# Attention and a gated unit on one core: K and Q loaded as one tile of nine tokens a partition, engines from a list, and a last output tile in quarters

## The chip, the cores and the metric

One core of a Trainium2 chip. The metric is the time of one execution on the device in microseconds; lower is better. The core has five engines with a queue of instructions each: TensorE (PE; its weight loads are listed apart as PEld), VectorE (DVE), ScalarE (ACT), GpSimd (POOL) and SyncE (SP), which here issues the transfers, and 16 DMA engines that carry them out. PE writes to PSUM, eight banks of 128 partitions x 512 fp32; all else is in SBUF, 128 partitions.

## What is computed

```python
def _attn_ref(q, k, v):                    # 8 batches, 8 heads, 576 positions, 64 dims, fp32
    scores = scale * np.matmul(q, k.transpose(0, 1, 3, 2))
    mask = block_i >= block_j              # blocks of 64 positions
    attn = np.exp(np.where(mask, scores, -1e9) - row_max);  attn /= attn.sum(-1)
    return np.matmul(attn, v)

def _moe_ref(x, w_val, conv_w, w_out):     # x: (8, 576, 512); conv_w: (5, 512)
    for k in range(5): gate_pre += conv_w[k] * xp[:, k:k + S, :]     # causal, along positions
    return (sigmoid(gate_pre) * (x @ w_val)) @ w_out
```

The attention's output, the eight heads side by side as 512 columns, goes through a depthwise convolution of five taps, a sigmoid gate, and two projections of 512 x 512.

## The kernel before

Work goes by 32 *pairs* of heads, four to a batch. Each step is an entry in a `Planner` (lines 40 to 166): the engines that may do it with a cost for each, its needs, and the PSUM banks that it holds. PE's steps stand in the order of the string `ORDER` (line 21), written out beforehand; `plan()` walks through all engines with the costs and gives every other step the engine that would be done with it first, and a place in that engine's queue. So the program that is built has a fixed order for each engine. Letters of `ORDER`, with the lines of what they emit:

- **T** (`transposes`, 326): K and Q of a pair, cast to fp16, are turned so that dims lie on partitions, 16 transposes of 64 rows for positions 0 to 511 and 2 for the *tail*, positions 512 to 575.
- **S** (`scores`, 375), three to a pair: scores by blocks, the masked ones left out, 22 matmuls in all. ACT takes exp of each two banks (`exps`, line 415, 128 x 1024).
- **P** (`products`, 438): 30 matmuls of 65 columns, V with a column of ones. DVE takes the reciprocal of the sums (463) and multiplies (473).
- **X** (`xt_steps`, 479): ten transposes back, evicted by `evict_x` (496). **G** (`gate`, 502): the convolution as 20 matmuls with diagonal weights, then tanh on ACT (519). **V** (`val`, 524), eight to a batch: x @ w_val, multiplied with the gate on DVE (`gated`, 540).
- **O** (`out_tile`, 546): 18 tiles of 128 output positions, each 16 matmuls of 512 columns into two banks, evicted with a factor 0.5 (`evict_out`, 563, 128 x 1024) and stored (574); a tile that crosses a batch's edge is stored in two pieces of its rows. **f** is a flag over the sums' range, **c** the convolution weights' transposes.

Loads go through SP in the planner's order (the first of Q through ACT). For a pair: K and Q of positions 0 to 511, each 128 partitions x 2 heads x 4 consecutive positions, so runs of 1 KB (262); V as two loads in runs of 256 B (303). For a batch: three tails of eight heads in runs of 256 B (310): K's to partitions 0-63, Q's to 64-127, V's. w_val and w_out come in eight loads into borrowed buffers (719), and the second half of w_out by a copy within SBUF (729). Rings: 5 raw tiles, 4 casts, 5 transposed K/Q tiles, 3 output buffers (`NOB`). Casts to fp16 stand at line 317: K's and Q's, V's and the tails' on POOL, but for the first pair or two. The transposed K is evicted with a stride of 64 elements on the PSUM side (357), since a partition holds four positions; Q needs none, as its transposes write to strided places (366). X therefore uses a permuted identity (`perm16`, 274). On POOL alone also stand a copy of a K block (`dup`), of a probability block (`keep_last`, 422), and two clearings of masked halves (`zeros`, 434).

The last steps: five O one after another, then f; the last O is evicted in two halves of 128 x 512, each stored by itself. Behind everything the flag is read, and a branch to an exact path (`exact_path`) that these data do not take.

Of the kernel before, what the change touches and what calls it, by code (L numbers as in the profile page):

```python
# [21 lines left out]
    "TTSTTSSSSTSSSSTPScXSPTSGPSTXSSPSSTSGXPGSSXTXPSGGXSSPSTGXSSTSGPSVVVVTSSVVVXVSTSPS"  # L22
    "SPVVVVXSPVVGTSXVVSSPGGXTSXGTSSGPSVVSSTVSVXSVVSTSPPSSVVTSPXXGGSXGGTSPSSVVVVXSTSPS"
    "SOSTOXSOSTPPSSVVVXSTGVSSXPGSTSPGGSTOSTOXSVVVVVTSSPPXSGGXSVVXSSOSTVVVSSPGGSTSPPSS"
    "VVVVVVXSOSTOSTOXXOSSPPGGGTSSOXSOSSOSPPPXXVVVXXVVVVGGGGGVVVVVVVVVOOOOOf")
# [14 lines left out]
class Planner:  # L40


    def __init__(self):
        self.steps = []

    def add(self, kind, key, engines, emit, needs=(), mode=None, banks=0, size=None, apart=False):
        s = Step(kind, key, engines, emit, needs, mode, banks, size, apart)
        s.n = len(self.steps)
        self.steps.append(s)
        return s  # L50

    def rank(self):
# [13 lines left out]
        for s in reversed(self.steps):  # L66
            if "PE" not in s.engines:
                s.rank = s.held.rank + 7 if s.held is not None else len(ORDER)
        changed = True
        while changed:  # L70
            changed = False
            for s in self.steps:
                for d in s.needs:
                    if "PE" not in d.engines and d.rank > s.rank:
                        d.rank = s.rank
                        changed = True

    def plan(self):
# [15 lines left out]
        def release(s):  # L94
            s.at = max([0.0] + [d.land for d in s.needs])
            if "PE" in s.engines:
                s.engine, s.ready = "PE", True
                return
            s.engine = min(s.engines, key=lambda e: (max(free[e], s.at) + s.engines[e], e))
            ready[s.engine].append(s)  # L100
# [69 lines left out]
def kernel(  # L170
# [46 lines left out]
    perm16 = ring(1, [128, 64], fp16, "perm16")[0]  # L217
# [6 lines left out]
    NRAW, NC, NT, NV, NPT, NX, NXT, NTH, NOB = 5, 4, 5, 6, 4, 3, 3, 9, 3  # L224
# [3 lines left out]
    tail32 = ring(2, [128, 8, 64], fp32, "tail32")  # L228
    tail16 = ring(2, [128, 8, 64], fp16, "tail16")
# [4 lines left out]
    kqs = ring(NT, [128, 1280], fp16, "kq")  # L234
# [23 lines left out]

    def load_runs(engine, src, t, b, j):
        engine.dma_start(
            out=t[:, :, :, :].rearrange("p e t d -> p e (t d)"),
            in_=src[b, 2 * j:2 * j + 2, 0:512, :].rearrange("e (p t) d -> p e (t d)", t=4))

    load_runs(nc.sync, k, raws["k"][0], 0, 0)
    load_runs(nc.scalar, q, raws["q"][0], 0, 0)
# [4 lines left out]
    for r in range(2):  # L272
        rows = slice(64 * r, 64 * r + 64)
        nc.vector.tensor_copy(out=perm16[rows, :].rearrange("p (s t) -> p t s", t=4),
                              in_=ident[rows, rows].rearrange("p (t s) -> p t s", t=4))
# [6 lines left out]
    RUN = {1024: 290.0, 256: 185.0, 2048: 340.0}  # L282
# [8 lines left out]
    def load_qk(p, name):  # L291
        b, j = divmod(p, PPB)
        src, t = {"k": k, "q": q}[name], raws[name][p % NRAW]
        return load(p - 4 + (0.1 if name == "q" else 0),
                    lambda _: load_runs(nc.sync, src, t, b, j), 262144, RUN[1024],
                    before(p - NRAW, "c" + name), 470)

    def load_v(p, e):
        b, j = divmod(p, PPB)
        t = raws["v"][p % NRAW]  # L300
# [7 lines left out]
    def load_tail(b, src, t, rows, users):  # L308
        def emit(_):
            nc.sync.dma_start(out=t[rows, :, :],  # L310
                              in_=src[b, :, 512:576, :].rearrange("h p d -> p h d"))

        return load(PPB * b - 3.8, emit, 131072, RUN[256], users, 650)

# [6 lines left out]
    def cast_engines(p, name):  # L321
        if p == 0:
            return {"DVE": 430} if name == "k" else {"ACT": 600}
        return {"POOL": 613} if p > 1 else {"POOL": 613, "DVE": 430}

    def transposes(p, parts):
        b, j = divmod(p, PPB)
        c16 = {n: casts[n][p % NC] for n in ("k", "q")}
        t16 = tail16[b % 2]

        def emit(s):
            i = s.group[0]
            for name, at in (("k", 320), ("q", 64)):
                if name not in parts:
                    continue
                for t in range(4):
                    for r in range(2):
                        rows = slice(64 * r, 64 * r + 64)
                        o = ps16[:, i + r, at:at + 256]
                        if name == "k":  # L340
                            o = o[:, 64 * t:64 * t + 64]
                        else:
                            o = o.rearrange("p (n t s) -> p t n s", t=4, s=16)[:, t, :, :]
                        nc.tensor.transpose(out=o, in_=c16[name][rows, t, :, :],  # L344
                                            identity=ident16[rows, rows])
            for r in range(2):
                rows = slice(64 * r, 64 * r + 64)
                if "t" in parts:
                    nc.tensor.transpose(out=ps16[:, i + r, 0:64], in_=t16[rows, 2 * j:2 * j + 2, :],  # L349
                                        identity=ident16[rows, rows])  # L350

        return emit

    def evict_k(p, tr):
        def emit(s):
            i = tr.group[0]
            copier(s.engine)(  # L357
                out=kqs[p % NT][:, 768:1280].rearrange("p (r s t) -> p r s t", r=2, t=4),
                in_=ps16[:, i:i + 2, 320:576].rearrange("p r (t s) -> p r s t", t=4))

        return emit

    def evict_q(p, tr, lo, hi):
        def emit(s):
            i = tr.group[0]
            copier(s.engine)(  # L366
                out=kqs[p % NT][:, 128:768].rearrange("p (r x) -> p r x", r=2)[:, :, lo:hi],
                in_=ps16[:, i:i + 2, lo:hi])

        return emit  # L370
# [4 lines left out]
    def scores(p, c):  # L375
        K = kqs[p % NT]
        TWICE, ZERO, KEYS, LAST = 0, 64, 768, 448

        def emit(s):
            i = s.group[0]  # L380

            def group(off, key, q0, n, start=True, stop=True):
                for e in range(2):
                    r = slice(64 * e, 64 * e + 64)
                    mm(out=ps[:, i + e, off:off + n], lhsT=K[r, key:key + 128],
                       rhs=K[r, q0:q0 + n], start=start, stop=stop)

            def both_halves(off, key):
                for e in range(2):
                    r = slice(64 * e, 64 * e + 64)  # L390
                    mm(out=ps[:, i + e, off:off + 512], lhsT=K[r, key:key + 128],
                       rhs=K[r, 128:768].rearrange("p (h x) -> p h x", h=2)[:, :, 64:320])

            if c == 0:
                both_halves(0, KEYS)
            elif c == 1:
                group(0, KEYS + 128, 320, 128)
                group(128, KEYS + 128, 512, 256)
                group(384, TWICE, 640, 64, stop=False)
                group(384, ZERO, LAST, 64, start=False)  # L400
                group(448, KEYS + 384, 704, 64)
            else:
                group(0, KEYS + 256, 512, 256)
                for tt in range(4):
                    group(256 + 64 * tt, KEYS + 128 * tt, LAST, 64)
# [14 lines left out]
    def keep_last(p):  # L420
        def emit(_):
            nc.gpsimd.tensor_copy(  # L422
# [5 lines left out]
    def zeros(p, first):  # L428
        def emit(_):
# [4 lines left out]
            nc.gpsimd.memset(seg[:, :, :, 0:64], 0.0)  # L434
# [44 lines left out]
    def xt_steps(p):  # L479
        def emit(s):  # L480
            for c in range(5):
                for r in range(2):
# [4 lines left out]
                        identity=perm16[rows, :] if c < 4 else ident16[rows, rows])  # L487
# [58 lines left out]
    def out_tile(i):  # L546
        def emit(s):
            for n in range(8):
                for e in range(2):
                    rows = slice(64 * e, 64 * e + 64)  # L550
                    mm(out=ps[:, s.group[0] + e, :], lhsT=gv[rows, n, 128 * i:128 * i + 128],
                       rhs=w_out_sb[rows, n, :], start=(n == 0), stop=(n == 7))
# [3 lines left out]
    def evict_out(n, ot, half=None):  # L556
        h = slice(0, 2) if half is None else slice(half, half + 1)

        def emit(s):
            i = ot.group[0]  # L560
            o, x = obs[n % NOB][:, h, :], ps[:, i + h.start:i + h.stop, :]
# [7 lines left out]
    def store(n, b, x0, x1, half=None):  # L569
        at = HALF * (b % UNIT) - 128 * (n % TILES)  # L570
        h = slice(0, 2) if half is None else slice(half, half + 1)

        def emit(_):
            nc.sync.dma_start(
                out=out[b, :, :].rearrange("(e s) n -> s e n", e=2)[x0:x1, h, :],
                in_=obs[n % NOB][at + x0:at + x1, h, :])
# [8 lines left out]

    def holds(s, *users):
# [3 lines left out]
    def memsets(key, engines, todo):  # L590

        def emit(s):
            e = {"DVE": nc.vector, "POOL": nc.gpsimd}[s.engine]
            for t, x in todo:
                e.memset(t, x)
# [26 lines left out]
    first = {n: add("", -4, {e: 0}, lambda _: None, size=(262144, RUN[1024]))  # L622
# [344 lines left out]
```

## Time and profile before

| | |
|---|---|
| median of 3 runs | 195.76 us (193.81 to 197.12) |
| the profiled execution | 194.38 us, of which the span of instructions is 192.6 us |
| busy: PE / DVE / ACT / POOL | 168.8 / 120.4 / 132.1 / 101.1 us |
| first matmul, first V step, last matmul | 4.5, 43.0, 184.3 us |
| mean granted clock of TensorE | 0.986 |

Times in the profile are microseconds from the span's start. A group's row has: line, engine, operation, out<-in with partitions x elements and type, count, then busy time, mean ns of one, and the idle time of the engine just before with what ended it. A timeline row: start, length, engine, line, operation, count. A row of the windows: the stretch and its length, busy time and count of PE, PEld, DVE, ACT and POOL, granted clock, mean busy share of the DMA engines (over 1 where packets overlap) and GB/s. Matmuls are pipelined, so the length of a matmul row reaches into the next; the time from start to start is the price.

### The profile page before, as it was taken

To read this page: it belongs to the slowest core of one execution; us is meant where nothing else is said; L and a number is where in the kernel's file an instruction comes from. 1 tells how busy PE (TensorE), PEld (TensorE's weight loads), DVE (VectorE), ACT (ScalarE), POOL (GpSimd) and SP (SyncE) were. 2 spreads that over 40 slices of the span, in tenths; PEclk is the share of its full clock that TensorE was granted. 3 is DMA by queue.
4 is the path that set the end of the run, shared out by engine and by line. 5 is a ranking of instruction groups with operands and counts; after the bars stand their busy time and mean duration, and the time that the engine had idled before them with its cause. 6 is when DMAs were issued, how large, how long until landed. Compare 5 with 4: busy or idle time off the path is not lost.

```text
span 192.6 us, 9420 instructions
## 1 busy us (share of the span) xinstructions
PE 168.8 (88%) x4006; PEld 127.4 (66%) x4006; DVE 120.4 (63%) x271; ACT 132.1 (69%) x151; POOL 101.1 (53%) x251
## 2 busy tenths in 40 slices
PE   0678789989999979997999979999999999999930
PEld 0357667868887758866577847868855858886410
DVE  6727877599798868958449727846944524965000
ACT  3398597995729978687787947798667997061540
POOL 4296977857855668774866855659642121000000
PEclk9999999999999999999999999999999999999995
DMA  5999998999998899999999999999837425200692
GB/s 153 315 235 171 285 233 221 277 331 185 233 252 189 239 212 228 234 205 206 228 226 238 300 348 264 245 299 331 194 122 245 181 90 145 101 3 3 158 333 67
DMA packets 70633, 41.05 MB, mean 213 GB/s; under 512 B 48053, under 2 KB 64949, under 8 KB 70586
## 3 DMA queue, kind: packets, MB, share of 16 engines
q1 hardware_dynamic: 70314, 40.13, 82.9%
q8 instruction: 33, 0.54, 1.2%
q10 hardware_dynamic: 272, 0.26, 0.4%
q14 instruction: 14, 0.11, 0.2%
HBM read 30.42 MB, written 9.44 MB: 207 GB/s over the span
## 4 chain that ended last, share of the span: by engine, by line
PE 52%; DMA 24%; ACT 6%; DVE 5%; POOL 5%; issue 3%; SPq 2%; POOLq 0%; ACTq 0%; DVEq 0%
PE ps L195 47%; DMA tail<-in_q_dram 8%; DMA qraw<-in_q_dram 8%; ACT pt L415 4%; DMA vraw<-in_v_dram 4%; DMA kraw<-in_k_dram 2%; DMA out_dram<-ob 2%; PE ps L344 2%; PE ps L484 2%; POOL ve L317 2%; ACT ob L563 2%; DVE xn L473 1%; DVE kq L357 1%; POOL qc L317 1%; DVE kq L366 1%
## 5 line engine op out<-in xcount | busy, mean ns | idle before, releaser
L415 ACT ACTIVATE pt<-ps 128x1024 f16<-128x1024 f32 x96 | 94.0, 1026 | 28.4 <-PE ps L195 20.1
L195 PE MATMUL ps<-kq 64*128 64x64 f16 (+3 forms) x704 | 36.4, 233 | 2.1 <-DVE kq L366 1.9
L357 DVE COPY kq<-ps 128x512 f16<-128x512 f16 x32 | 22.1, 690 | 23.5 <-PE ps L349 18.8
L195 PE MATMUL ps<-ve,pt 128*128 128x65 f16 x896 | 33.5, 195 | 2.7 <-POOL ve L317 1.7
L195 PE MATMUL ps<-xt,w_val 128*64 128x288 f16 x512 | 35.4, 288 | 0.3 <-DVE xn L473 0.3
L195 PE MATMUL ps<-w_out,gv 64*128 64x512 f16 x288 | 33.4, 376 | 1.2 <-ACT pt L415 1.2
L195 PEld LDWEIGHTS <-pt 128*128 128x128 f16 x896 | 30.8, 98 | 5.1 <-issue 2.0
L195 PEld LDWEIGHTS <-w_val 128*64 128x64 f16 x512 | 27.4, 110 | 4.7 <-issue 2.1
L195 PEld LDWEIGHTS <-kq 64*128 64x128 f16 x704 | 23.1, 98 | 11.1 <-issue 4.3
L540 DVE SCALAR_TENSOR_TENSOR gv<-th,ps 128x288 f16<-128x288 f32 x64 | 27.7, 452 | 4.0 <-ACT th L519 1.5
L519 ACT ACTIVATE th<-ps 128x576 f32<-128x576 f32 x32 | 20.2, 653 | 10.5 <-PE ps L195 10.4
L473 DVE TENSOR_TENSOR xn<-ps,rinv 128x640 f16<-128x640 f32 x32 | 26.3, 823 | 1.0
L563 ACT ACTIVATE ob<-ps 128x1024 f32<-128x1024 f32 (+1 forms) x19 | 18.5, 980 | 11.8 <-PE ps L195 9.4
L195 PE MATMUL ps<-xt,diag 64*64 64x288 f16 x640 | 23.5, 285 | 0.7 <-ACT pt L415 0.7
L195 PEld LDWEIGHTS <-gv 64*128 64x128 f16 x288 | 13.5, 94 | 15.1 <-issue 1.5
L434 POOL MEMSET pt<- 64x256 f16 x64 | 19.7, 312 | 5.6 <-ACT pt L415 4.0
L317 POOL CAST ve<-vraw 128x512 f16<-128x512 f32 x32 | 19.5, 614 | 4.7 <-DMA vraw<-in_v_dram 3.5
L317 POOL CAST kc<-kraw 128x512 f16<-128x512 f32 x30 | 18.4, 614 | 5.1 <-DMA kraw<-in_k_dram 3.9
L317 POOL CAST qc<-qraw 128x512 f16<-128x512 f32 x30 | 18.3, 612 | 4.8 <-DMA qraw<-in_q_dram 3.1
L422 POOL COPY pd<-pt 64x128 f16<-64x128 f16 x32 | 9.6, 299 | 20.8 <-ACT pt L415 20.0
L496 DVE COPY xt<-ps 128x640 f16<-128x640 f16 x31 | 14.9, 485 | 7.1 <-PE ps L484 6.9
L195 PEld LDWEIGHTS <-diag 64*64 64x64 f16 x640 | 17.1, 106 | 2.9 <-issue 1.1
(53 smaller groups left out, 143.4 us busy)
## 6 DMA issues: line engine op xcount, KB each, us to landing
kraw<-in_k_dram SPq DMA_DIRECT2D x32, 256.0 KB, 5.1
vraw<-in_v_dram SPq DMA_DIRECT2D x64, 128.0 KB, 5.1
qraw<-in_q_dram SPq DMA_DIRECT2D x31, 256.0 KB, 5.6
out_dram<-ob SPq DMA_DIRECT2D x11, 512.0 KB, 3.4
out_dram<-ob SPq DMA_DIRECT2D x4, 384.0 KB, 4.2
out_dram<-ob SPq DMA_DIRECT2D x6, 256.0 KB, 4.7
tail<-in_k_dram SPq DMA_DIRECT2D x8, 128.0 KB, 5.3
tail<-in_q_dram SPq DMA_DIRECT2D x8, 128.0 KB, 5.3
```

The source lines that it names most:

```text
L195: nc.tensor.matmul(out=out, lhsT=lhsT, rhs=rhs, start=start, stop=stop, skip_group_check=True)
L317: copier(s.engine)(out=out, in_=in_)
L344: nc.tensor.transpose(out=o, in_=c16[name][rows, t, :, :], identity=ident16[rows, rows])
L357: copier(s.engine)(out=kqs[p % NT][:, 768:1280].rearrange("p (r s t) -> p r s t", r=2, t=4), in_=ps16[:, i:i + 2, 320:576].rearrange("p r ...
L415: nc.scalar.activation(out=heads(p)[:, :, 512 * c:512 * c + 512], in_=ps[:, i:i + 2, :], func=AF.Exp, bias=0.0, scale=0.125)
L422: nc.gpsimd.tensor_copy(out=pds[p % NPT][64:128, 0:128].rearrange("p (e x) -> p e x", e=2), in_=heads(p)[64:128, :, COL[3]:COL[3] + 64])
L434: nc.gpsimd.memset(seg[:, :, :, 0:64], 0.0)
L473: nc.vector.tensor_tensor(out=xns[p % NX][:, :, :, :].rearrange("p c e d -> p e c d"), in0=o[:, :, :, 0:64], in1=ri.to_broadcast([128, 2, ...
L496: copier(s.engine)(out=xts[b % NXT][:, g, PAD:PAD + 640].rearrange("p (c r x) -> p r c x", r=2, x=64), in_=ps16[:, i:i + 2, 0:320].rearran ...
L519: nc.scalar.activation(out=ths[p % NTH][:, :, :], in_=ps[:, i:i + 2, 0:HALF], func=AF.Tanh, bias=0.0, scale=0.5)
L540: nc.vector.scalar_tensor_tensor(out=gv[:, 2 * g + r, s0:s0 + HALF], in0=ths[(PPB * b + g) % NTH][:, r, :], scalar=1.0, in1=ps[:, va.group ...
L563: nc.scalar.activation(out=o, in_=x, func=AF.Copy, bias=0.0, scale=0.5)
```

## The change

- **One tile for K and Q.** K goes to partitions 0-63, Q to 64-127, each partition with nine consecutive positions (64 x 9 = 576), in runs of 2304 B; the tails of K and Q go (16 loads of 128 KB), V's stay. One cast a pair of 128 x 1152 elements instead of two of 512 and a share of the tail's (for the first pair K's on DVE, Q's on ACT). T is again 18 transposes of 64 rows. Both evictions are now 128 x 576 with a stride, on DVE or ACT, and put positions back in order, so `perm16` goes and the scores take queries in one piece: two matmuls of 128 and 256 columns for each head become one of 384, 20 matmuls a pair.
- **Engines from a list.** A step that more than one engine may do takes it from the string `CHOICE` (320 letters) and not from the planner. `keep_last`, `zeros`, `dup` and V's casts may now be DVE's; `evict_kq` and the output evictions are shared. Counts in the built programs:

| | before | after |
|---|---|---|
| K/Q casts | POOL 60, DVE 3, ACT 1, tails 8 | POOL 22, DVE 10, ACT 1 |
| K/Q evictions | DVE 65 | DVE 43, ACT 21 |
| xt evictions | DVE 31, ACT 1 | DVE 23, ACT 9 |
| V casts / `dup` / `keep_last` / `zeros` on DVE | none | 12 / 11 / 15 / 31 |
| output evictions | ACT 17 + 2 halves | ACT 7 + 1 quarter, DVE 10 + 3 quarters |
| transfers of K and Q with tails | 64 + 16 | 64 |

- **A new `ORDER`**, with 122 changes between forms of matmul where there were 118. The first V stands at place 47, before at place 63; ahead of it stand 9 T, 23 S, 6 P, 4 X and 4 G, before 12, 28, 8, 7 and 7. In SP's queue 16 loads of K or Q and 14 of 256 B runs stand ahead of the last of w_val, before 20 and 24.
- **The end.** The last O becomes two steps of 256 columns, evicted in quarters of 128 x 256, each stored by itself (128 KB). f is now ahead of them, and they need the flag. `NOB` is 4.

```diff
+CHOICE = ("PADPDDDDDDDDPPPDDPDDDPPDPDPP..." )
...
+        s.engine = next(iter(engines))
+        if len(engines) > 1:
+            s.engine = {"D": "DVE", "A": "ACT", "P": "POOL"}[CHOICE[self.choices]]
+            self.choices += 1
...
-            s.engine = min(s.engines, key=lambda e: (max(free[e], s.at) + s.engines[e], e))
...
-    raws = {n: ring(NRAW, [128, 2, 4, 64], fp32, n + "raw") for n in ("k", "q", "v")}
-    casts = {n: ring(NC, [128, 4, 2, 64], fp16, n + "c16") for n in ("k", "q")}
+    raws = ring(NRAW, [128, 2, 9, 64], fp32, "kqraw")
+    casts = ring(NC, [128, 9, 2, 64], fp16, "kq16")
+    vraws = ring(NRAW, [128, 2, 4, 64], fp32, "vraw")
...
+    def load_runs(engine, n, t, b, j):
+        engine.dma_start(
+            out=t[64 * n:64 * n + 64, :, :, :].rearrange("p e t d -> p e (t d)"),
+            in_=(k, q)[n][b, 2 * j:2 * j + 2, :, :].rearrange("e (p t) d -> p e (t d)", t=9))
...
+            for t in range(9):
+                for r in parts:
+                    rows = slice(64 * r, 64 * r + 64)
+                    nc.tensor.transpose(
+                        out=ps16[:, s.group[0] + r - parts[0], 64 * t:64 * t + 64],
+                        in_=casts[p % NC][rows, t, :, :], identity=ident16[rows, rows])
...
+    def evict_kq(p, tr, n, bank):
+            copier(s.engine)(
+                out=kqs[p % NT][:, at:at + 576].rearrange("p (s t) -> p s t", t=9),
+                in_=ps16[:, tr.group[0] + bank, 0:576].rearrange("p (t s) -> p s t", t=9))
...
-                group(0, KEYS + 128, 320, 128)
-                group(128, KEYS + 128, 512, 256)
+                group(0, K0 + 128, 2, 384)
...
+            P["c0"] = P["c1"] = cast(p, None, {"POOL": 1280, "DVE": 760}, [P["l0"], P["l1"]])
...
+            P[f"e{n}"] = add("", p, {"DVE": 757, "ACT": 655},
+                             evict_kq(p, P[f"t{n}"], n, n if p else 0), [P[f"t{n}"]] + users)
...
+            for cols in (slice(0, 256), slice(256, 512)) if last else (slice(0, 512),):
+                o = add("O", p, {"PE": 870 if last else 1727}, out_tile(i, cols),
+                        need + lo + ([sf] if last else []), "A", 2)
...
+                for h in halves:
+                    ev = add("", p, {"ACT": 385, "DVE": 420} if last else {"ACT": 1027, "DVE": 1160},
+                             evict_out(n, o, h, cols), [o] + old)
```

More of the change, by code (lines that the diff above doesn't have):

```diff
@@ L65, in rank @@
         assert len(self.pe) == sum(len(x) for x in queues.values())
-        for s in reversed(self.steps):
+        for s in self.steps:
             if "PE" not in s.engines:
                 s.rank = s.held.rank + 7 if s.held is not None else len(ORDER)
[L69 to L76, printed above, removed]
+        for s in reversed(self.steps):
+            for d in s.needs:
+                if "PE" not in d.engines:
+                    d.rank = min(d.rank, s.rank)
     def plan(self):
@@ L319, in copy_step, with cast @@
         return add("", key, engines, emit, needs)
[L321 to L324, printed above, removed]
+    def cast(p, n, engines, needs):
+        rows = slice(0, 128) if n is None else slice(64 * n, 64 * n + 64)
+        return copy_step(p - 2, engines, casts[p % NC][rows, :, :, :].rearrange("p t e d -> p e t d"),
+                         raws[p % NRAW][rows, :, :, :], needs + before(p - NC, "t0", "t1"))
@@ L486, in emit @@
                         in_=xns[p % NX][rows, c, :, :],
[L487 removed]
+                        identity=ident16[rows, rows])
         return emit
@@ L745 @@
                 T["val"].append([va])
+        if b == B - 1:
+            cs = add("", NP, {"DVE": 1400}, check_sums, [pairs[x]["xn"] for x in range(NP)])
+            mf = add("f", NP, {"PE": 200}, make_flag, [cs], "C", 1)
+            sf = add("", NP, {"DVE": 140}, set_flag, [mf])
+            holds(mf, sf)
         u, bi = divmod(b, UNIT)
@@ L780, in make_flag @@
-    def make_flag(s):
-        mm(out=ps[0:1, s.group[0], 0:1], lhsT=allr[:, :], rhs=ones[:, :])
-    def set_flag(_):
-        nc.vector.tensor_scalar(out=flag[:, :], in0=ps[0:1, mf.group[0], 0:1], scalar1=127.5,
-                                scalar2=None, op0=ALU.is_lt)
-    cs = add("", NP, {"DVE": 1400}, check_sums, [pairs[x]["xn"] for x in range(NP)])
-    mf = add("f", NP, {"PE": 200}, make_flag, [cs], "C", 1)
-    sf = add("", NP, {"DVE": 140}, set_flag, [mf])
-    holds(mf, sf)
+            halves = (slice(0, 1), slice(1, 2)) if last else (slice(0, 2),)
```

269 lines of the change are left out of this document (105 added, 164 removed).

## The prediction

> **What bounds the kernel now.** I read the page first, then the windows by stage, the timeline of dense stretches for the price of each TensorE step, the groups by form, and the waits.
>
> ```profile
> span 192.6 us, 9420 instructions
> PE 168.8 (88%) x4006; PEld 127.4 (66%) x4006; DVE 120.4 (63%) x271; ACT 132.1 (69%) x151; POOL 101.1 (53%) x251
> DMA packets 70633, 41.05 MB, mean 213 GB/s; under 512 B 48053, under 2 KB 64949, under 8 KB 70586
> q1 hardware_dynamic: 70314, 40.13, 82.9%
> ```
> ```profile
> 4.50:43.00 38.50, 31.90 (x834) 25.04 (x834) 26.50 (x55) 30.17 (x35) 27.07 (x65) 1.00 1.05 258
> 43.00:128.00 85.00, 80.64 (x2034) 61.99 (x2034) 62.41 (x131) 63.35 (x73) 56.65 (x132) 1.00 1.03 239
> 128.00:184.40 56.40, 56.12 (x1142) 40.34 (x1138) 28.43 (x63) 35.85 (x41) 15.21 (x40) 1.00 0.50 154
> 184.40:192.60 8.20, 0.11 (x2) 0.00 (x1) 0.14 (x1) 1.23 (x3) 0.00 (x0) 0.66 0.51 176
> ```
>
> Columns of the second fence: stretch and length, busy time of PE, weight loads, DVE, ACT, POOL, granted clock, DMA share, GB/s. PE works almost without a gap from 43 us on; the DMA engines are full (1.05, 1.03) until 128 us, and half empty after. The clock is full to the end of PE's work, so it plays no part. Busy PE time holds hidden waits, so I price the steps where they follow each other without a wait:
>
> ```profile
> 25.06 0.60 PE L195 MATMUL ps<-ve,pt 128*128 128x65 f16 x14 [0.37 <-DVE kq L366]
> 26.08 0.39 PE L195 MATMUL ps<-kq 64*128 64x512 f16 x2
> 43.02 2.15 PE L195 MATMUL ps<-xt,w_val 128*64 128x288 f16 x32
> 140.12 0.42 PE L195 MATMUL ps<-kq 64*128 64x128 f16 x10
> 142.10 0.39 PE L195 MATMUL ps<-kq 64*128 64x256 f16 x10
> 142.32 0.28 PE L344 MATMUL ps<-ident,kc 64*128 64x64 f16 x8
> 142.59 1.89 PE L195 MATMUL ps<-w_out,gv 64*128 64x512 f16 x16
> 144.31 0.38 PE L195 MATMUL ps<-kq 64*128 64x512 f16 x2
> 146.52 0.28 PE L484 MATMUL ps<-perm,xn 64*128 64x64 f16 x8
> 146.66 0.28 PE L484 MATMUL ps<-perm,xn 64*128 64x64 f16 x8
> 160.19 0.60 PE L195 MATMUL ps<-ve,pt 128*128 128x65 f16 x14
> 161.11 0.59 PE L195 MATMUL ps<-ve,pt 128*128 128x65 f16 x14
> 167.85 3.26 PE L195 MATMUL ps<-xt,diag 64*64 64x288 f16 x100
> ```
>
> From start to next start: transposes of a pair (T) 142.59-142.32 = 0.27 us, the scores (S) 0.22, 0.25 (140.12 to the next step at 140.37) and 0.22, X 0.14, an output tile (O) 1.72, products (P) 161.11-160.19 = 0.92, a gate (G) 3.26/5 = 0.65, a value step (V) 2.08/4 less one change = 0.50. A lone P took 26.08-25.06 = 1.02, so a change of matmul form costs 0.10; ORDER has 118. Sum: 32 x (0.27+0.69+0.92+0.14+0.65+1.00) + 18 x 1.72 + 11.8 = 160.2 us. PE runs from 4.5 to 184.4, 179.9 us: 19.7 us of waits. Up to the first V at 43.0 ORDER holds 25.9 us of work in 38.5: 12.6 us of waits. After it 134.4 in 141.4: 7. What can be won is these, and the 8.2 us behind PE's end.
>
> **The change, part by part.** *Loads.*
>
> ```profile
> DMA packets 188, 0.39 MB, mean 385 GB/s; under 512 B 0, under 2 KB 0, under 8 KB 188
> ```
>
> A store's 2 KB packet on all rows takes 1.02 x 16 us / 188 = 87 ns (the 158.00 row below, and its packet count here); a straight line through it and the whole, 82.9% of 16 x 192.6 us, gives 26 ns for 256 B, 52 ns for 1 KB, 95 ns for 2304 B. K and Q of a pair with their share of the tails are now 512 x 52 + 256 x 26 = 33.4 us of engine time, 2.1 us on 16; after, 256 x 95 = 24.4, or 1.5 us. V and its tail stay, 1.9. But K goes to rows 0-63 alone and Q to 64-127, and no load of this kind is in the trace. The nearest are stores of half the rows: output tile 13 crosses a batch and leaves as two pieces of 64 rows.
>
> ```profile
> 179.60:181.20 1.60, 1.60 (x18) 0.68 (x14) 0.00 (x0) 0.90 (x2) 0.00 (x0) 1.00 0.80 155
> 158.00:159.00 1.00, 1.00 (x21) 0.59 (x17) 0.00 (x0) 1.00 (x2) 0.18 (x1) 1.00 1.02 385
> 129.50:131.50 2.00, 2.00 (x49) 1.64 (x46) 1.92 (x5) 1.46 (x3) 1.94 (x6) 1.00 1.03 334
> ```
>
> Alone (first row) two such pieces move 155/0.80 = 194 GB/s of busy time, against 385/1.02 = 377 for 128 rows; another such pair mixed with K and Q loads (third row) does not hurt: 334. So a 2304 B packet costs between 95 and 95 x 377/194 = 185 ns. I take 125, nearer the mixed row, since V loads stand between most pairs of K and Q: 2.0 us a pair, so I count no gain in DMA time. The Trainium skill (SBUF — State Buffer, Door 1: The DMA port swizzle) says that 64 partitions reach only 8 of 16 ports, as 32 do, and that two transfers on the two halves gain 6%. The stores agree (194 against 377); by it the high end holds, which is the last rival.
>
> *The front.* The first V needs w_val. Before its last load stand 20 K/Q loads and 24 loads of 256 B: (20 x 256 x 52 + 24 x 512 x 26 + 512 x 87)/16 = 39.4 us, from 2 us on: 41.4, where the row of 41.40 below has the last casts. After, 16 loads of K or Q and 14 of 256 B stand there: (16 x 128 x 125 + 186,000 + 44,500)/16 = 30.4, so 32.4 us (28.6 at 95 ns, 40 at 185). ORDER puts only 19 us of PE work ahead of V, not 25.9. In ACT's list 22 exps, three tanhs and three evictions stand ahead of it, 22 x 0.98 + 6 x 0.66 = 25.5 us (rows below), from about 7.6: the first scores come near 7, a little later than now, since the casts of K and Q are over twice as long, 1152 elements for 512. That makes 33.1, the later of the two; I set the first V at 33.2.
>
> *Engines.* Prices:
>
> ```profile
> L415 ACT ACTIVATE pt<-ps 128x1024 f16<-128x1024 f32 x96 | 94.0, 1026 | 28.4 <-PE ps L195 20.1 <-POOL pt L434 2.5 <-DVE gv L540 2.5
> L357 DVE COPY kq<-ps 128x512 f16<-128x512 f16 x32 | 22.1, 690 | 23.5 <-PE ps L349 18.8 <-ACT pt L415 3.6 <-PE ps L344 0.5
> L366 DVE COPY kq<-ps 128x640 f16<-128x640 f16 x31 | 14.9, 481 | 0.0
> L473 DVE TENSOR_TENSOR xn<-ps,rinv 128x640 f16<-128x640 f32 x32 | 26.3, 823 | 1.0
> L519 ACT ACTIVATE th<-ps 128x576 f32<-128x576 f32 x32 | 20.2, 653 | 10.5 <-PE ps L195 10.4
> L563 ACT ACTIVATE ob<-ps 128x1024 f32<-128x1024 f32 x17 | 17.4, 1025 | 11.6 <-PE ps L195 9.4 <-DMA out_dram<-ob 1.5 <-ACT pt L415 0.5
> L317 POOL CAST kc<-kraw 128x512 f16<-128x512 f32 x30 | 18.4, 614 | 5.1 <-DMA kraw<-in_k_dram 3.9 <-PE ps L195 0.3
> L317 POOL CAST ve<-vraw 128x512 f16<-128x512 f32 x32 | 19.5, 614 | 4.7 <-DMA vraw<-in_v_dram 3.5
> ```
> ```profile
> 39.53 0.61 POOL L317 CAST ve<-vraw 128x512 f16<-128x512 f32 x1
> 39.61 0.82 DVE L317 CAST w_val<-ob 128x512 f16<-128x512 f32 x1
> 41.40 1.19 DVE L317 CAST w_val<-ob 128x512 f16<-128x512 f32 x3
> ```
>
> DVE loses the two evictions of a pair (32 x 0.69 + 31 x 0.48 = 37), casts, the perm tile, 8 x 0.48 of xt: 47 us in all. It gains 43 strided evictions of 576 (0.69 to 0.78, taken 0.76: 32.6), 10 casts of 1152 (0.76 to 0.95: 8), 12 V casts (0.42: 5), 26 small copies and 31 memsets (estimate 0.18: 10), 10 output tiles (1.2, by 823 ns for 640 elements from PSUM: 12) and three quarter tiles (1.3): 69. So DVE goes from 120 to about 142 us. ACT gains 21 evictions of 576 at 0.65, 8 of xt, 1 longer cast and gives 10 output tiles: 132 to 141. POOL drops to about 70 (22 casts between 1.14 and 1.38). From first V to the 40th V, DVE's list sums to 80 us beside 88 us of PE work; before, the fullest stretch was 0.93 to 0.95.
>
> DVE's copies also collide with POOL: the cast at 39.61 took 0.82 against 0.40 for those at 41.40, since POOL's cast ran until 40.14. The Trainium skill (SBUF — State Buffer, Who interferes with whom) has it that a DVE copy between SBUF tiles and a GpSimd operation exclude each other for a whole instruction; the 0.4 us agree. Of 31 such copies in that stretch about half meet POOL (70 of some 130 us busy), with about 0.4 us left of its operation: 0.2 on average, 6 us, so DVE is at 86 of 88. I charge 7% of 88, 6.2 us of waits (before 5% at 0.93), and 1.6 in the last 53.4 us of PE work, 0.45 of it because the last tile now waits for the flag. If a copy waited 0.8 each time (a whole new cast), DVE would be at 105. Merged scores save between 0 and 1.6 us (two of ten matmuls of 0.25 us, 32 times; 0.4 taken), four more changes of form cost 0.4. The longer store ring frees the 1.47 us wait of an eviction, which nobody waited for but the stores.
>
> *The end.*
>
> ```profile
> 175.58 8.81 PE L195 MATMUL ps<-w_out,gv 64*128 64x512 f16 x80
> 184.57 2.11 SPq L574 DMA_DIRECT2D out_dram<-ob  x3
> 184.82 1.09 ACT L563 ACTIVATE ob<-ps 128x512 f32<-128x512 f32 x2 [0.28 <-DMA out_dram<-ob]
> out_dram<-ob SPq DMA_DIRECT2D x4, 128.0 KB, 3.8
> ```
>
> Now: PE's end 184.35, two half evictions one after the other until 185.91, the last store issued until 186.68. After: two quarter evictions on DVE and ACT (0.42 by 594 ns for twice the size) end 0.65 behind PE, two issues of 0.4, and a landing of 3.8 as now: 1.8 us less, 6.4 instead of 8.2.
>
> **Sum.** 33.2 + 88 + 6.2 + 53.4 + 1.6 = 182.4; plus 6.4 is a span of 188.8. The profiled execution took 194.38 us for 192.6, so 190.6; the median of the runs is 195.76. I say 190.5.
>
> **The rivals.**
> *More is won* (20%): after the first V PE waits only as before (5% of 88, 1 us at the end) and w_val comes at 29: 190.5 - 1.8 - 0.6 - 2 = 186. For it: POOL is freed and 3.9, 3.1 and 3.5 us of its casts' waits for loads go. Against: DVE and ACT both near 90%.
> *Given back* (29%): V starts early, then evictions hold PE. At 0.4 us for each of 31 copies DVE needs 92 of 88 us; with the 7% on top PE's stretch is 98, 4 us longer, and late casts push the first V by another 1 to 2: 196. The row at 39.61 speaks for it.
> *Slower* (19%): half-row loads at the rate of half-row stores. At 185 ns a pair needs 3.0 + 1.9 = 4.9 us; 32 pairs, and 17 us for weights and some stores, end at 174. The same sum for the kernel before, 32 x 4.0 + 17, is 145, where the DMA share falls at about 130: so 174 stands for 157 or so. The last T stands 33 us of PE work ahead of 182, at 149, and needs its load 3 us earlier: 11 to 14 us late, 203. It decides from about 160 ns a packet. Against it: the mixed row, and that K and Q are two halves that can be in flight together.
> My forecast keeps 32%, the largest share.
>
> **Numbers.** Likeliest 190.5, its own range 187 to 193. 2% is about what this kernel's runs (193.81 to 197.12) can tell from no change: below 191.8 faster, above 199.7 slower. Faster 0.52 (20 and the forecast's 32), same 0.29, slower 0.19. The range, 184.5 to 199.5, leaves out most of the last rival.
>
> **What would show it.** The first w_val matmul at 31 to 35 us; last DVE casts of w_val just ahead. A K or Q load to landing under 6 us, the DMA share below 1 after 60 us; a window of K and Q loads alone near 200 GB/s would mean the slow rival. DVE copies from kqraw, vraw and pt longer than 0.76, 0.42 and 0.2 where POOL is busy. DVE busy near 142, ACT 141, POOL 70. PE's last matmul to span end 6.4 us. The prediction fails if T steps wait for POOL's or DVE's cast all through (DMA behind), or if the first V comes after 38 us.

## The result, and the profile after

| | before | after |
|---|---|---|
| median | 196.44 us (193.81 to 198.35) | 218.28 us (215.93 to 222.02) |
| profiled execution, its span | 194.38, 192.6 us | 222.02, 220.2 us |
| busy: PE / DVE / ACT / POOL | 168.8 / 120.4 / 132.1 / 101.1 | 177.6 / 146.6 / 140.4 / 70.9 us |
| first V step, last matmul | 43.0, 184.3 us | 39.0, 212.6 us |

The change makes the kernel 11% slower: the ratio of the times is 1.112, with a 95% interval of 1.097 to 1.126. The profiled execution of the changed kernel is the longest of its runs (granted clock 0.95; the shortest, 215.93 us, had 0.984), so its trace, long waits and clock drops included, shows up to 6 us more of a loss than another run has.

Head of the page of the changed kernel:

```profile
span 220.2 us, 9216 instructions
PE 177.6 (81%) x3958; PEld 133.3 (61%) x3958; DVE 146.6 (67%) x320; ACT 140.4 (64%) x170; POOL 70.9 (32%) x143
DMA packets 54281, 41.05 MB, mean 186 GB/s; under 512 B 39637, under 2 KB 40661, under 8 KB 54234
q1 hardware_dynamic: 54090, 40.10, 84.9%
```

The windows by stage (to the first V, to the last loads' landing, to the end of PE's work, behind it), columns as in the prediction:

```profile
4.50:39.00 34.50, 25.59 (x600) 19.86 (x602) 27.33 (x56) 25.62 (x30) 13.56 (x26) 1.00 1.10 222
39.00:154.00 115.00, 93.43 (x2191) 70.87 (x2190) 79.75 (x165) 79.91 (x97) 49.62 (x85) 0.94 1.12 224
154.00:213.00 59.00, 58.57 (x1176) 42.52 (x1172) 37.49 (x81) 33.34 (x42) 5.54 (x18) 0.97 0.31 97
213.00:220.20 7.20, 0.00 (x0) 0.00 (x0) 0.35 (x1) 0.07 (x1) 0.00 (x0) 0.67 0.52 179
```

There are 16,000 packets less and the same 41 MB, but the DMA engines are full (1.12) until 154 us where they were full until 128, at 224 GB/s for 239 in the longest window of before. PE has gaps as long as loads come (busy 93 of 115 us) and nearly none after. Who waits for the loads is shown by a group and the issues (size, median us to landing):

```profile
L320 POOL CAST kq<-kqraw 128x1152 f16<-128x1152 f32 x22 | 25.4, 1157 | 17.4 <-DMA kqraw<-in_q_dram 14.3
```
```profile
kqraw<-in_k_dram SPq DMA_DIRECT2D x32, 288.0 KB, 7.2
kqraw<-in_q_dram SPq DMA_DIRECT2D x31, 288.0 KB, 7.5
vraw<-in_v_dram SPq DMA_DIRECT2D x64, 128.0 KB, 7.1
```

A K or Q load lands 7.2 to 7.5 us behind its issue, a V load 7.1, and POOL's 22 casts stand still for 14.3 us until Q is there. Of the two signs that the prediction named for its failure, one is there: the first V starts at 38.97 us. The other, T steps waiting for casts all through, is not: behind the first T they wait 3.0 us for casts in all. PE's longest waits are of another kind, taken up at the end.

```profile
38.97 1.92 PE L201 MATMUL ps<-xt,w_val 128*64 128x288 f16 x24
```

### The profile page after: what moved, and what is told of

The parts are those of the page before. It is cut to its first block, busy times and chain, and to the rows that moved or that the text cites. A ratio compares the mean times of both kernels' runs of the same rounds, so it can differ in the third digit from the quotient of the medians.

```text
span 220.2 us, 9216 instructions
## 1 busy us (share of the span) xinstructions
PE 177.6 (81%) x3958; PEld 133.3 (61%) x3958; DVE 146.6 (67%) x320; ACT 140.4 (64%) x170; POOL 70.9 (32%) x143
## 3 DMA queue, kind: packets, MB, share of 16 engines
q1 hardware_dynamic: 54090, 40.10, 84.9%
## 5 line engine op out<-in xcount | busy, mean ns | idle before, releaser
L201 PE MATMUL ps<-xt,w_val 128*64 128x288 f16 x512 | 38.3, 302 | 4.0 <-issue 3.2
L346 DVE COPY kq<-ps 128x576 f16<-128x576 f16 x43 | 31.3, 753 | 13.7 <-PE ps L335 13.3
L201 PE MATMUL ps<-w_out,gv 64*128 64x512 f16 (+1 forms) x304 | 33.6, 365 | 0.4 <-DVE xn L445 0.4
L201 PEld LDWEIGHTS <-kq 64*128 64x128 f16 x640 | 21.4, 99 | 16.5 <-issue 7.1
L320 POOL CAST kq<-kqraw 128x1152 f16<-128x1152 f32 x22 | 25.4, 1157 | 17.4 <-DMA kqraw<-in_q_dram 14.3
L335 PE MATMUL ps<-ident,kq 64*128 64x64 f16 x576 | 15.7, 200 | 12.1 <-DVE kq L320 7.5
L335 PEld LDWEIGHTS <-kq 64*128 64x128 f16 x576 | 12.3, 101 | 16.4 <-DVE kq L320 7.8
L537 DVE TENSOR_SCALAR ob<-ps 128x1024 f32<-128x1024 f32 (+1 forms) x13 | 13.4, 1038 | 8.8 <-PE ps L201 8.8
L346 ACT COPY kq<-ps 128x576 f16<-128x576 f16 x21 | 13.2, 645 | 7.9 <-PE ps L335 7.9
L394 POOL COPY pd<-pt 64x128 f16<-64x128 f16 x17 | 6.2, 362 | 36.9 <-ACT pt L387 36.7
L406 POOL MEMSET pt<- 64x256 f16 x33 | 11.0, 335 | 19.9 <-ACT pt L387 17.8
```

The costliest lines, as they stand in the source:

```text
L201: nc.tensor.matmul(out=out, lhsT=lhsT, rhs=rhs, start=start, stop=stop, skip_group_check=True)
L320: copier(s.engine)(out=out, in_=in_)
L335: nc.tensor.transpose(out=ps16[:, s.group[0] + r - parts[0], 64 * t:64 * t + 64], in_=casts[p % NC][rows, t, :, :], identity=ident16[rows, ...
L346: copier(s.engine)(out=kqs[p % NT][:, at:at + 576].rearrange("p (s t) -> p s t", t=9), in_=ps16[:, tr.group[0] + bank, 0:576].rearrange("p ...
L394: copier(s.engine)(out=pds[p % NPT][64:128, 0:128].rearrange("p (e x) -> p e x", e=2), in_=heads(p)[64:128, :, COL[3]:COL[3] + 64])
L406: setter(s.engine).memset(seg[:, :, :, 0:64], 0.0)
```

## The experiments

The theory after the result, called *rows*: a load that writes half of the partitions moves at half the rate, also when the other half's load stands right behind it. Its rivals: *engines* (DVE and ACT, with more to evict and their collisions with POOL, hold PE), *runs* (2304 B runs are slow wherever they go), and *queue* (two halves would go together if two queues issued them).

**The loads alone (`rates`).** Nine stretches of loads without any other work, one call for each form:

```python
kq[i][64*n:64*n+64, ...] <- k or q, "e (p t) d -> p e (t d)", t=9      # 1, 4: half rows; 3: Q's on ACT's queue
kq[i][:, 576*n:576*n+576] <- k or q, "e (p t) d -> (e p) (t d)", t=9   # 2: all rows
kq[i][:, 512*n:512*n+512] <- k or q, "e (p t) d -> p e (t d)", t=4     # 5: the form of before
```

> Loads alone, no attention: nine stretches, each of 8 pairs and each behind the last: (1) half-row loads of 2304 B runs, K to rows 0-63, then Q to 64-127, on SP's queue as in the changed kernel; (2) the same bytes and runs on all 128 rows; (3) as 1, with Q's loads on ACT's queue; (4) K's half-row loads alone; (5) the kernel before's loads, 128 rows in runs of 1 KB; (6) V's loads alone; (7) to (9) forms 1, 2 and 5 with V's loads between. The output is zeros. Theory 'rows' (a load that reaches half the partitions gets half the rate): 1 and 4 near 200 GB/s, 2 near 377, and 3 no better than 230. Rival 'queue' (K and Q halves hinder each other only because one queue takes them one after the other): 1 and 4 near 200, 3 above 300. Rival 'runs' (2304 B runs are slow on any rows): 2 also near 220, 5 above 2. Mixed with V the rows theory gives 4.9 us a pair for 7 and about 3.5 for 8.

The windows of that kernel, one inside each stretch in the order of the list (columns: stretch, length, busy time of DVE and of POOL, granted clock, DMA share, GB/s):

```profile
20.00:28.00 8.00, 8.00 (x38) 0.00 (x0) 1.00 1.05 230
32.50:37.50 5.00, 5.00 (x22) 0.00 (x0) 1.00 1.05 391
54.00:61.00 7.00, 4.12 (x10) 0.00 (x0) 1.00 1.04 224
65.00:73.00 8.00, 5.54 (x15) 0.00 (x0) 1.00 1.05 213
80.00:88.00 8.00, 7.00 (x14) 0.00 (x0) 1.00 1.10 349
92.00:98.00 6.00, 4.82 (x14) 0.00 (x0) 1.00 1.30 217
102.00:128.00 26.00, 9.08 (x25) 0.00 (x0) 1.00 1.18 216
135.00:151.00 16.00, 9.40 (x31) 0.00 (x0) 1.00 1.07 311
156.00:172.00 16.00, 8.48 (x20) 0.00 (x0) 1.00 1.11 289
```

The engines are full in each, so the last column is the rate of the form. The same bytes in the same runs go at 391 GB/s on all rows and at 213 on one half. K and Q halves in turn on one queue reach 230, on two queues 224: that is 5 to 8% over one half alone, and *queue* falls. *Runs* falls too: 2304 B on all rows are faster than 1 KB (349). A 2304 B packet takes 2304 x 16 x 1.05 / 391 = 99 ns on all rows, 168 with K and Q halves in turn, 182 on one half alone. With V's loads between, the form of the change moves 216 GB/s, all rows 311: the 852 KB of a pair take 3.9 us for 2.7, both less than the 4.9 and 3.5 that I expected. The Trainium skill (DMA: Bandwidth & Descriptors, Rules for kernel authors) says of two transfers to disjoint halves that they share the same engines and serialize, from one queue or from two; 230 and 224 against 391 agree.

**The changed kernel with loads on all rows (`all_rows`).**

```diff
-            out=t[64 * n:64 * n + 64, :, :, :].rearrange("p e t d -> p e (t d)"),
-            in_=(k, q)[n][b, 2 * j:2 * j + 2, :, :].rearrange("e (p t) d -> p e (t d)", t=9))
+            out=t[:, n, :, :].rearrange("p t d -> p (t d)"),
+            in_=(k, q)[n][b, 2 * j:2 * j + 2, :, :].rearrange("e (p t) d -> (e p) (t d)", t=9))
```

> The changed kernel with one edit: K's load of a pair fills the first half of the tile's free space on all 128 rows (head 0 on rows 0-63, head 1 on 64-127) and Q's the second half. Same bytes, same 2304 B runs, same number of transfers and the same instructions elsewhere; K and Q of the heads are mixed up, so it computes another attention. Theory 'rows': a K/Q load lands in under 6 us, the DMA share falls under 1 ahead of 135 us, 186 to 194 us. Rival 'engines' (DVE and ACT, with the evictions, casts and collisions that CHOICE gives them, hold TensorE): 210 us or more, as changed. Rival 'runs': also 210 or more, with K/Q loads still over 7 us.

(The casts of the first pair now also wait for both loads.) 193.09 us, 0.985 of the kernel before (0.978 to 0.991): the edit takes 25 us away, and with the packets as large and as many as in the change. A K or Q load lands in 5.2 to 5.7 us, as expected. Page and windows (to the first V, to the last loads' landing, to PE's end, behind it):

```profile
span 191.4 us, 9217 instructions
PE 169.5 (89%) x3958; PEld 129.2 (68%) x3958; DVE 144.9 (76%) x320; ACT 139.7 (73%) x170; POOL 72.3 (38%) x143
q1 hardware_dynamic: 54090, 40.10, 75.5%
```
```profile
4.50:35.80 31.30, 25.53 (x599) 20.10 (x600) 26.19 (x56) 25.43 (x30) 14.26 (x26) 1.00 1.06 293
35.80:124.00 88.20, 83.90 (x2088) 64.89 (x2084) 75.83 (x160) 74.99 (x91) 46.09 (x79) 1.00 1.03 274
124.00:184.00 60.00, 60.00 (x1284) 44.21 (x1280) 40.87 (x86) 37.38 (x48) 9.76 (x24) 1.00 0.29 92
184.00:191.40 7.40, 0.05 (x2) 0.00 (x0) 0.42 (x1) 0.38 (x1) 0.00 (x0) 0.70 0.55 189
```

The 54,090 packets of the queue take 75.5% of 191.4 us, 144.5 us on each engine, where they took 84.9% of 220.2, or 187. DVE, ACT and POOL do the same work as in the change, and PE idles 21.9 us of the span, not 42.6. *Engines* does not hold for the loss.

**The changed kernel without most loads (`no_loads`).**

```diff
-        ... lambda _: load_runs(nc.sync, n, raws[p % NRAW], b, j), 294912,
+        ... lambda _: load_runs(nc.sync, n, raws[p % NRAW], b, j) if p < NRAW else None, 294912,
```

> The changed kernel with the K and Q loads of pairs 5 to 31 left out: the raw tiles of pairs 0 to 4 are cast again, so it computes another attention; all other instructions and their order stay. It shows what the engines alone take. Theory 'rows': 182 to 190 us, my sum of the prediction with its waits. Rival 'engines': 205 us or more. If it is 190 to 205, both have a share.

194.62 us, 0.996 of before (0.991 to 1.000): no faster than with all loads on all rows, and 5 us above the upper end of what I expected. The same window as the second one above:

```profile
35.80:124.00 88.20, 84.74 (x2113) 65.57 (x2110) 76.67 (x163) 75.77 (x93) 46.29 (x80) 1.00 0.50 122
```

With the DMA engines half empty (0.50) PE is busy 84.7 of 88.2 us, with them full 83.9. So once loads go at full rate they cost next to nothing behind the front. That this kernel is no faster as a whole fits its first V, at 37.5 us for 35.8: its first five pairs still come by half rows.

**Half rows in the kernel before (`before_by_rows`, `before_by_heads`).** Each K or Q load is issued as two, by rows or by heads:

```diff
+        for r in (slice(0, 64), slice(64, 128)):        # by rows
+                out=t[r, ...], in_=src[...].rearrange("e (p t) d -> p e (t d)", t=4)[r, :, :])
+        for e in range(2):                              # by heads
+                out=t[:, e, ...], in_=src[b, 2 * j + e, 0:512, :].rearrange("(p t) d -> p (t d)", t=4))
```

> The kernel before with one edit: each K or Q load of 128 rows is issued as two, rows 0-63 and rows 64-127 (same bytes, same 1 KB runs, twice the transfers). Theory 'rows': 524 KB of a pair's K and Q take 2.5 us at 212 GB/s for 1.5 at 348, some 30 us more of DMA time in all, the loads end 25 to 30 us later, and the time is 212 to 226 us. Rival 'issues' (what costs is the number of transfers in SP's queue): as slow as the split by heads.

> The control to the split by rows: each K or Q load of the kernel before is issued as two, one for each head, both on all 128 rows. Same bytes, runs and number of transfers as the split by rows. Theory 'rows': within 2% of the kernel before, 194 to 199. Rival 'issues': as slow as the split by rows, 205 or more.

By rows: 226.74 us, 1.171 of before (1.165 to 1.178). By heads: 205.04 us (201.78 to 205.32), for which no interval is to be had, beside 193.98 for the kernel before. The control missed its 194 to 199, so the times do not tell what the pair was made for. The windows of 60 to 90 us, the issues on the tile (duration of an issue in ns: min/median/max) and the queue's packets with their share of the span, by rows and then by heads:

```profile
60.00:90.00 30.00, 25.13 (x570) 19.27 (x571) 19.69 (x44) 17.91 (x21) 16.20 (x38) 0.89 0.76 196
L263 SPq DMA_DIRECT2D kraw<-in_k_dram x64: 595/605/1912, 0.8 to 163.3; - x64
q1 hardware_dynamic: 71322, 40.13, 67.2%
```
```profile
60.00:90.00 30.00, 27.44 (x734) 20.99 (x729) 23.39 (x49) 22.64 (x27) 19.59 (x46) 1.00 0.85 217
L263 SPq DMA_DIRECT2D kraw<-in_k_dram x64: 327/436/1700, 0.8 to 143.0; - x64
q1 hardware_dynamic: 71322, 40.13, 73.5%
```

In both the DMA engines are no longer full (0.76, 0.85), which points to SP's issuing as the limit. An issue of half the rows takes 0.605 us at the median, one of all rows 0.436, and 126 of them at 0.17 more are 21 us, about as much as by rows is slower than by heads (21.7 us between the medians, 25 to the fastest run by heads). In the changed kernel this is not what binds, since its engines are full (1.12).

The packets speak against *rows* here. They take 67.2% of 224.1 us by rows, 150.6 us on each engine, and 73.5% of 203.3, or 149.4, by heads: the 30 us more that I expected are not there, and a time close to my range came from elsewhere. So *rows* is shown for runs of 2304 B one behind the other with the engines full, and not for runs of 1 KB. A half of 128 KB every 0.605 us is 217 GB/s, about the rate of half rows in `rates`, so the split may never have asked half rows for more than they give; that was not tried.

**All rows, with the reference's attention (`two_pairs`, `late_flag`).** K of pairs p and p+1 share a tile, one on each half, and Q of the pairs p and p+1 for odd p, so that K and Q of a pair still lie on different halves for T. `late_flag` also reads the flag behind all stores.

```diff
+            out=raws[m % NRAW][:, e, :, :].rearrange("p t d -> p (t d)"),
+            in_=(k, q)[n].rearrange("b (j e) (s t) d -> e (b j) s (t d)", e=2, t=9)[e, p:p + 2, :, :])
```
```diff
-        if n == min(ends + 6, len(order) - 1):
+        if n == len(order) - 1:
```

> The changed kernel with its loads put on all 128 rows and the right result: a tile holds K of two pairs, p and p+1 (p even), one on each half of the rows, or Q of two pairs (p odd); each of its two loads takes one head of both pairs, 128 rows x 2304 B. K of a pair and its Q still lie on different halves, so transposes, evictions, casts and their engines stay as they are. Theory 'rows': as with all rows and mixed heads, 191.5 to 194.5 us, about 1.4% faster than the kernel before. Rival 'later casts': a pair now needs two casts of two tiles, one of them from the step before, and a cast tile is held for two pairs, so TensorE waits for casts again: 195.5 to 200.

> As two_pairs, and the flag is read behind all stores, where the kernel before reads it, instead of six steps behind the flag. In the traces of the changed kernel SP reads the flag for 1.1 us between the first and the second of the last four stores. Theory: that read is the tail's missing 0.9 us, so this is 0.7 to 1.3 us faster than two_pairs. Rival: the last store lands when it does because of its own 4 us, or the read behind the stores costs the same again: within 0.3 us of two_pairs.

476.79 us, 2.46 of before, and 477.49: both theories missed. A window of `two_pairs` in which hardly anything else moves:

```profile
20.00:24.00 4.00, 0.00 (x0) 0.00 (x0) 0.00 (x0) 1.36 (x2) 0.00 (x0) 1.00 0.13 51
```

The DMA share is 0.13, which is 2 of 16 engines, at 51 GB/s. The two heads of the source lie two heads apart, so its outermost count is 2. The Trainium skill (DMA: Bandwidth & Descriptors, Why a DMA increments its semaphore by 16 and not by 1) says that a transfer runs on the largest number of engines up to 16 that divides the outermost counts of both sides; the share of 0.13 agrees. On the flag nothing can be read from this pair.

**All rows, from one run of memory (`split_pairs_early`, `split_pairs`, `split_pairs_2`).** Of heads h0 to h3 the pairs are now (h0, h2) and (h1, h3); a load takes two neighbouring heads, 128 x 2304 B, and a T turns K (or Q) of two pairs.

```diff
+    def head(g, r):
+        return 4 * (g // 2) + g % 2 + 2 * r
+            out=raws[m % NRAW][:, e, :, :].rearrange("p t d -> p (t d)"),
+            in_=(k, q)[m % 2][b, h:h + 2, :, :].rearrange("r (p t) d -> (r p) (t d)", t=9))   # h = 4u + 2e
...
-    "ADDAPPDDDDD..."                                    # CHOICE, split_pairs
+    "DDADPPDDDDD..."                                    # split_pairs_2: the first T's evictions
```

> The changed kernel with the right result and K/Q loads of 128 rows that are one run of memory: of each four heads h0 to h3 the pairs are (h0, h2) and (h1, h3), a tile holds K (or Q) of both pairs, rows 0-63 h0 and h2, rows 64-127 h1 and h3, so each of its two loads takes two neighbouring heads, 128 x 2304 B. One T turns K of two pairs, the next their Q (32 T, one place of ORDER less); w_val's rows come in halves in the order of the new pairs, and the convolution's weights are sorted by a copy on POOL. Theory 'rows' with the source's outer count repaired: 192 to 196 us, as with all rows and mixed heads but for 1 to 2 us of w_val's eight half loads ahead of the first V. Rival 'later casts': a T needs a tile with two pairs, so loads are wanted one pair earlier and TensorE waits: 197 to 205. If the two-pair load was slow for another reason than its outer count of 2, over 300.

> As split_pairs_early, and the flag is read behind all stores, where the kernel before reads it. In the trace of the changed kernel SP reads the flag for 1.1 us between two of the last four stores. Theory: this is 0.7 to 1.3 us faster than split_pairs_early, 191 to 195 us. Rival: the read costs the same behind the stores: within 0.3 us.

> As split_pairs, with two letters of CHOICE changed: both evictions of the first T go to DVE. In split_pairs ACT evicts K of the second pair at 7.46 us ahead of its cast of the first Q, which ends only at 9.15, and the first scores start at 10.71 (7.68 with all rows and mixed heads). Now that cast starts when Q has landed, by 6.5, and ends by 7.7: scores near 9, the first V 1 to 2 us earlier than 38.2, and the time 193 to 194.7 us, 1% under the kernel before. Rival: the front has slack, since w_val's half loads set the first V: no change, 195.5.

196.04 us, 1.003 of before (0.998 to 1.007); 195.50 with the late flag, 1.001 (0.997 to 1.005); 193.79 with the two letters, 0.995 (0.992 to 0.999). So a source of one run repairs the 477 us, and the last form is faster than both kernels, than the kernel before by 0.5%. (Its edit is three letters: the second T's two evictions change places as well.) The front has a part: the first V comes at 38.2 us in `split_pairs`, where two pairs must be loaded and cast before the first score, and at 37.8 in `split_pairs_2`, where the first score starts at 8.86 us and not at 10.71:

```profile
8.86 1.09 PE L201 MATMUL ps<-kq 64*128 64x512 f16 x10 [0.72 <-ACT kq L352]
37.82 1.66 PE L201 MATMUL ps<-xt,w_val 128*64 128x288 f16 x24
```

Of the 1.9 us at the first score 0.4 are left at the first V, and the time to before falls by 0.6%. Whether the rival has a part is not shown: the last of w_val's half loads is issued at 29.9 us, in `all_rows` at 25.9, but PE comes to the first V straight from the step before it. What binds between is not taken apart.

**The flag (`all_rows_late_flag`).** The same edit as in `late_flag`, on `all_rows`.

> The changed kernel with all rows and mixed heads (another attention, as in all_rows), and the flag read behind all stores. Theory: the last stores leave 1 us earlier, 191.8 to 192.6 us for 193.1. Rival: the wait moves behind the stores and stays in the span, 193.

193.27 us, 0.990 of before (0.986 to 0.994), beside 193.09: nothing is won. With the split pairs it is 0.5 us between the medians, and the two intervals overlap. The rival holds.

## Why the prediction was wrong, step by step

*What bounds the kernel now* held in the main: with the loads repaired, waits of PE are what a new layout can win or lose. But not all of the 12.6 us ahead of the first V were waits (see the front).

*Loads: "I take 125, nearer the mixed row, since V loads stand between most pairs of K and Q: 2.0 us a pair".* This step failed. The packet takes 168 ns with K and Q in turn and 182 alone, near the upper of my two ends (185), and 590 KB of a pair take 2.6 us, not 2.0. V's loads between do not help: 216 GB/s with them. The mixed row that I leaned on (129.50 to 131.50, 334 GB/s) was misread: SP only issues the two half-row stores there, from 129.57 on, and they land 5.2 us behind their issue, while the store issued at 127.33 is one of all rows.

```profile
127.33 0.42 SPq L574 DMA_DIRECT2D out_dram<-ob  x1
129.57 1.65 SPq L574 DMA_DIRECT2D out_dram<-ob  x2
```

So that row shows in the main the rate of transfers on all rows. The low end, 95, was right for all rows (99), so the fit was sound and the choice between the ends was not. The row of stores alone (194 GB/s for 377) was the nearest in kind. By the rule of the Trainium skill that the prediction quotes (SBUF — State Buffer, Door 1: The DMA port swizzle), 64 partitions reach half the ports; 213 GB/s against 391 agree.

*The front: first V at 33.2.* It came at 38.97, and at 35.80 with loads on all rows. So 3.2 us are the loads. The other 2.6 lie with PE's own steps: I weighed w_val's loads against ACT's list and put PE's work ahead of V at 19 us, where `all_rows` has it busy for 25.5 (window above), from 5.78 us on and with some 4 us of short waits between. Four rows of its timeline:

```profile
12.73 0.96 PE L201 MATMUL ps<-ve,pt 128*128 128x65 f16 x14
24.09 0.58 PE L201 MATMUL ps<-ve,pt 128*128 128x65 f16 x14
31.27 0.39 PE L201 MATMUL ps<-kq 64*128 64x512 f16 x2 [0.92 <-ACT th L491]
35.80 0.68 PE L201 MATMUL ps<-xt,w_val 128*64 128x288 f16 x8
```

The last wait of PE that the timeline shows ahead of V ends at 31.27, and from there its steps follow each other up to 35.80, so V does not wait for w_val. The same 14 matmuls of a P take 0.96 us at 12.73 and 0.58 at 24.09; my prices came from dense stretches, the earliest at 25 us. The granted clock is 1.00 up to the first V, and what slows the first steps is not shown.

*Engines* was about right: DVE 146.6 us for 142, ACT 140.4 for 141, POOL 70.9 for 70. The groups of `all_rows` on DVE:

```profile
L346 DVE COPY kq<-ps 128x576 f16<-128x576 f16 x43 | 31.2, 752 | 6.2 <-PE ps L335 5.7
L320 DVE CAST ve<-vraw 128x512 f16<-128x512 f32 x12 | 7.0, 597 | 0.1
L394 DVE COPY pd<-pt 64x128 f16<-64x128 f16 x15 | 5.1, 337 | 3.3 <-ACT pt L387 3.0
```

The eviction takes 0.75 us for 0.76. Of the copies between SBUF tiles, V's casts take 0.60 for the 0.42 that I counted without POOL and `keep_last` 0.34 for 0.18: 0.16 to 0.18 more for each, close to the 0.2 us that I had for a collision. K/Q's casts, at 0.77, show hardly any of it. From the first V to PE's end `all_rows` takes 184.0 - 35.8 = 148.2 us; my 88 + 6.2 + 53.4 + 1.6 is 149.2.

*The end: 6.4 us.* From the last matmul to the end it is 7.6 in the changed kernel and 7.4 in `all_rows`. SP reads the flag between the last stores, which I had not seen; the answer on the flag's tile in `all_rows` has it (min/median/max ns, start):

```profile
L753 SPq TENSOR_LOAD <-flag x1: 1089/1089/1089, 184.6 to 184.6; - x1
```

But reading it later does not shorten the span (191.4 us in both), so what holds the last stores there stays open.

*The sum* for `all_rows`: 188.8 + 2.6 (front) - 1.0 + 1.0 (end) = 191.4, its span.

*The rivals.* The slower one named the price of a half-row packet and the point from which it decides (160 ns), and got 19%. Its 203 us was too low, and its path is not the one in the trace: it made the last T late by 11 to 14 us. PE falls behind `all_rows` in many small steps from the first T on, 28.5 us in all. Of these 8.1 are longer busy time for the same 3958 matmuls, at a clock of 0.94 in the long stretch, and 20.4 are idle time, some 3 of it ahead of the first V. What ended PE's waits in the changed kernel (us in total, times, the longest):

```profile
PE ps L201 <- issue: 12.1, 5, 3.6
PE ps L335 <- DVE kq L320: 7.5, 2, 6.6
PE ps L335 <- issue: 2.5, 2, 1.3
PE ps L335 <- POOL kq L320: 2.1, 3, 0.9
```

The T steps (L335) wait 3.0 us for casts, without the 6.6 ahead of the very first. "issue" means that PE waits for nothing that the profile shows. The two rows make 14.6 us, where such waits in `all_rows` come to 0.8. Three of them hold 9.7 us, each in the midst of a step:

```profile
55.94 0.38 PE L201 MATMUL ps<-ve,pt 128*128 128x65 f16 x4 [3.62 <-issue]
102.88 1.42 PE L201 MATMUL ps<-xt,diag 64*64 64x288 f16 x20 [2.86 <-issue]
153.75 1.49 PE L201 MATMUL ps<-xt,w_val 128*64 128x288 f16 x12 [3.24 <-issue]
```

So `all_rows` shows that the half-row loads cost the 25 us. By which path the full DMA engines hold PE is for the most part open: late casts are a small part of it in this trace.

## What to carry to other kernels

Count the partitions that a transfer reaches before its packets: here larger runs on 64 rows cost 25 us, the same runs on 128 rows none (shown for runs of 2304 B with full DMA engines). Where two rows of the trace disagree on a price, take the one that holds only that kind of transfer, and see when the transfers issued in a window land. See that a load's source has a large outermost count, or it runs on few DMA engines.

## What the runs showed of the hardware that I had not expected

- A load of 128 rows whose source is two blocks ran on 2 of 16 DMA engines (share 0.13, 51 GB/s, 477 us for the kernel).
- To issue a load of half the rows (64 rows of two runs) takes SP 0.60 us, one of all rows with the same 128 packets (128 rows of one run) 0.33 at least (0.605 and 0.436 at the median in the split kernels).
- Loads of 2304 B runs on all rows moved 391 GB/s, and V's 256 B runs 217, as slow as half rows.
- Behind each of the three long waits PE's granted clock drops for some microseconds, in the changed kernel's windows to 0.52, 0.77 and 0.72:

```profile
56.00:62.00 6.00, 6.00 (x102) 4.69 (x102) 3.21 (x6) 2.47 (x3) 1.80 (x4) 0.52 1.09 184
102.90:110.00 7.10, 7.10 (x118) 4.61 (x119) 2.77 (x5) 5.07 (x7) 2.35 (x4) 0.77 1.14 201
154.00:160.00 6.00, 6.00 (x98) 4.30 (x96) 3.61 (x9) 1.71 (x3) 0.00 (x1) 0.72 0.66 174
```

What PE waited for there is not shown. In each of the three a 16 KB packet of the program's instructions (33 in the whole run) ends 1.5 to 1.6 us before PE goes on, and with loads on all rows there is no such wait; that the code came late through the full DMA engines is argued from this, and was not tried.
